# K formed in pairs of steps, sums over rows in pairs, the last chunk's forward transform in column halves, and a new order

## The chip, the cores and the metric

The kernel runs on one core of a Trainium2 chip. The metric is the device time of one execution in microseconds (us), lower is better. The engines are TensorE (PE, whose weight loads are listed as PEld), VectorE (DVE), ScalarE (ACT), GpSimd (POOL), and SyncE (SP), which here issues nearly all transfers.

## The reference

Two state-space convolutions (S4) of the same input are mixed by a gate. L is 2048, D is 512, N is 128.

```python
def _A_ref(u, A_re, A_im, B_re, B_im, C_re, C_im, log_dt, Dskip):   # _B_ref is the same
    dt = jnp.exp(log_dt)[:, None]
    logdA = dt * (A_re + 1j * A_im)
    dB = dt * (B_re + 1j * B_im)
    P = jnp.exp(logdA[:, :, None] * l[None, None, :])
    K = jnp.einsum("dn,dnl,dn->dl", Cc, P, dB).real
    ...  # y = irfft(rfft(u padded to 2 L) * rfft(K padded to 2 L)), first L values
    y = y.transpose(0, 2, 1) + u * Dskip[None, None, :]
    return y

g = _sigmoid((x * gate_w).sum(-1, keepdims=True))
return g * a + (1 - g) * b
```

## The kernel before

Channels come in 8 chunks `c` of 64. A chunk holds its 64 channels for both convolutions, so 128 columns, the first 64 (`s` = 0) for A and the last 64 for B.

**Steps.** A chunk is made in 8 steps `T` of 16 columns, 64 steps in all. In each (`tables`), POOL writes two pieces of phases (`ang`) and two of magnitudes (`mr`, from the seeds `ml` and `mh`), ACT takes two sines and a square (`s`, `ang`, `sq`; `s` and `sq` lie in PSUM), and DVE makes from them the real table in place (`mr`) and the imaginary one (`ei`) with two instructions each (lines 277 and 287). In every fifth step DVE writes one piece of `mr` instead of POOL. PE then forms 4 x 32 rows of K in one PSUM bank (`kgen`, line 595), a copy of 256 values a row takes them to half of `kt`, and an addition of 4 columns puts the skip term in (`kt<-c,dsk`).

**Transforms.** After every second step `first` (line 612) does the first part of K's transform for 32 columns, and two copies put it into `xa` (even chunks) or `xb` (odd ones). When a chunk is complete, `spectrum` (line 625) does the second part in 8 blocks `j`, with the constants `w2` (named `w_0` to `w_3` in the order below), DVE multiplies with the input's spectrum `u` (line 701, result `y`), and `back` does the inverse for two blocks at a time, U = 0 to 3 (line 721). The result goes through `z` to `zb` in DRAM and back in another layout to `f`, for the last chunk to `xa`. The input's spectra were made in the same way at the start (`u_spectra`) and lie in DRAM (`us`).

**Ends.** `fin` (line 757) does the last sums over rows for a quarter `k` of a chunk with constants that carry the gate (`gsi`); a copy of 256 takes them to `o`, and a transfer of 128 KB writes them out. Near the end of the program `stay_awake` runs matmuls without use.

**Start.** The parameters are prepared for groups of one, three and four chunks (`prep`): transposes on PE, then arithmetic on DVE, with two rows on POOL (lines 469 and 498, into `par` or `vv`).

**What sets the order.** Every operation has a number, and the table `ORDER` lists all of them. A word with a `b` takes the second engine of those that it may use (copies: ACT or DVE; the pieces of `mr`: POOL or DVE). Each engine runs its instructions in the order of the table, and SP's transfers wait in line in the same way. Buffers of a ring are given out along the table: `ang` 2, `mr` 3, `ei` 2, `y` 3, `z` 2, `kt` 2, and `c`, 4 PSUM banks of 512 values a row that all matmul results but those in `s` and `sq` share. The last chunk's inverses go to `s` and `sq`, which the steps no longer need.

The functions as they stand before:

Of the kernel before, what the change touches and what calls it, by code (L numbers as in the profile page):

```python
# [207 lines left out]
def ssm_mix(ctx: ExitStack, tc: tile.TileContext, a, out, dry=False):  # L208
    slots, pools, shapes = {}, {}, {}

    def ring(tag, n, shape, dtype=F32, space=None):
# [646 lines left out]
```

## Time and profile before

| | us |
|---|---|
| median of 3 runs | 430.75 (429.98 to 430.92) |
| the profiled execution | 428.49 |
| its span, first to last instruction | 426.7 |
| PE, PEld busy in it | 385.4, 342.9 |
| DVE, ACT, POOL busy | 385.1, 361.4, 359.0 |
| granted TensorE clock | 1.000 |

Busy time is the union of an engine's instructions. An instruction can begin before the one ahead of it has ended, so the durations of a group add up to more than the time that it takes. PE's count of records is twice the count of matmuls in the code. A line named for POOL, DVE or ACT is that of a helper (`tt`, `stt`, `actv`, `copy`), so groups are told apart by their tiles. "Wait" names the engine and line that waited, then what ended the wait, and the us in total, the number and the longest.

### The profile page before, as it was taken

How to read it: one execution, taken by the hardware profiler on the slowest of the kernel's cores; microseconds unless marked ns; L12 is line 12 of the kernel's file. 1: busy time of each engine (PE TensorE's matmuls, PEld its weight loads, DVE VectorE, ACT ScalarE, POOL GpSimd, SP SyncE). 2: the span in 40 equal slices, each digit the busy share in tenths (PEclk: the TensorE clock that was granted, in tenths of full speed). 3: DMA queues.
4: the chain of work that ended last, by engine and by line, in shares of the span. 5: the costliest groups of instructions: out<-in, count | busy, mean ns of one | idle time of the engine just before them, and what ended most of it. 6: DMA issues, size and time to landing. Idle time of an engine off the chain costs nothing.

```text
span 426.7 us, 21919 instructions
## 1 busy us (share of the span) xinstructions
PE 385.4 (90%) x9636; PEld 342.9 (80%) x9636; DVE 385.1 (90%) x547; ACT 361.4 (85%) x522; POOL 359.0 (84%) x291
## 2 busy tenths in 40 slices
PE   5888887799998989999989999999889979999995
PEld 5787776688877878888989988888778968889964
DVE  5799999999999999999989999999999999996620
ACT  2889999999998999999889989999899897992211
POOL 1796999899999999998999999999999999970000
PEclk9999999999999999999999999999999999999999
DMA  8968855078783676588476555674767476567894
GB/s 234 298 207 275 243 169 180 28 230 221 252 248 84 195 228 184 157 243 254 127 226 178 176 173 146 172 232 131 203 220 216 148 233 197 173 196 221 232 269 137
DMA packets 79855, 84.63 MB, mean 198 GB/s; under 512 B 7600, under 2 KB 62768, under 8 KB 79664
## 3 DMA queue, kind: packets, MB, share of 16 engines
q1 hardware_dynamic: 79472, 82.96, 65.0%
q8 instruction: 76, 1.25, 1.2%
q10 hardware_dynamic: 288, 0.26, 0.2%
q14 instruction: 19, 0.16, 0.1%
HBM read 51.55 MB, written 31.65 MB: 195 GB/s over the span
## 4 chain that ended last, share of the span: by engine, by line
PE 34%; ACT 24%; DVE 11%; issue 10%; DMA 9%; POOL 7%; SPq 4%; ACTq 0%; DVEq 0%; POOLq 0%
PE c L612 9%; PE c L625 8%; PE c L595 6%; PE c L721 5%; SPq L295 4%; ACT s L290 4%; ACT sq L290 4%; PE c L757 3%; DVE mr L287 3%; ACT z L300 3%; ACT ang L290 3%; POOL ang L277 3%; DMA zb<-z 2%; POOL mr L277 2%; POOL sa L277 2%
## 5 line engine op out<-in xcount | busy, mean ns | idle before, releaser
L287 DVE SCALAR_TENSOR_TENSOR mr<-sq,mr 128x1024 f32<-128x1024 f32 (+1 forms) x128 | 117.5, 945 | 2.5 <-ACT sq L290 2.4
L277 POOL TENSOR_TENSOR mr<-ml 128x1024 f32<-128x1024 f32 x52 | 101.9, 1960 | 2.0 <-PE c L595 1.5
L277 DVE TENSOR_TENSOR ei<-s,mr 128x1024 f32<-128x1024 f32 x64 | 77.6, 1213 | 2.4 <-POOL mr L277 1.0
L595 PE MATMUL c<-mr 128*32 128x64 f32 x2048 | 64.9, 222 | 8.2 <-DVE mr L287 2.2
L290 ACT ACTIVATE s<-ang 128x1024 f32<-128x1024 int32 x64 | 66.2, 1034 | 5.7 <-DVE ei L287 3.2
L277 POOL TENSOR_TENSOR ang<-sa 128x512 int32<-128x512 int32 x64 | 70.2, 1098 | 0.3
L701 DVE TENSOR_TENSOR y<-c,u 128x1024 f32<-128x1024 f32 x57 | 68.7, 1213 | 1.5 <-PE c L625 1.2
L277 POOL TENSOR_TENSOR ang<-par,cint 128x512 int32<-128x512 int32 x64 | 67.5, 1057 | 2.5 <-ACT sq L290 2.5
L290 ACT ACTIVATE ang<-ang 128x1024 f32<-128x1024 int32 x64 | 67.9, 1060 | 0.9
L277 POOL TENSOR_TENSOR mr<-mh 128x512 f32<-128x512 f32 x64 | 68.6, 1076 | 0.0
L290 ACT ACTIVATE sq<-ang 128x1024 f32<-128x1024 f32 x64 | 66.1, 1033 | 2.9 <-DVE mr L287 1.5
L612 PE MATMUL c<-small,kt 128*64 128x128 f32 x1024 | 63.4, 275 | 2.4 <-ACT z L300 1.4
L595 PE MATMUL c<-ei 128*32 128x64 f32 x2048 | 63.8, 219 | 1.6 <-issue 1.6
L595 PEld LDWEIGHTS c<-mr 128*32 128x32 f32 x2048 | 49.0, 109 | 19.6 <-issue 10.3
L612 PEld LDWEIGHTS c<-small,kt 128*64 128x64 f32 x1024 | 55.6, 137 | 6.3 <-ACT z L300 1.9
L721 PE MATMUL c<-y,vv 64*64 64x128 f32 x1792 | 58.4, 273 | 2.3 <-issue 1.5
L625 PE MATMUL c<-xb,w 128*128 128x128 f32 x384 | 51.8, 283 | 5.1 <-DVE c L420 1.6
L721 PEld LDWEIGHTS c<-y,vv 64*64 64x64 f32 x1792 | 50.5, 133 | 6.9 <-issue 2.9
L625 PE MATMUL c<-xa,w 128*128 128x128 f32 x384 | 53.1, 285 | 3.0 <-ACT z L300 2.3
L625 PEld LDWEIGHTS c<-xb,w 128*128 128x128 f32 x384 | 45.6, 191 | 10.4 <-issue 2.0
L595 PEld LDWEIGHTS c<-ei 128*32 128x32 f32 x2048 | 50.8, 110 | 2.1 <-issue 2.1
L625 PEld LDWEIGHTS c<-xa,w 128*128 128x128 f32 x384 | 46.0, 191 | 7.7 <-ACT z L300 3.0
(108 smaller groups left out, 595.0 us busy)
## 6 DMA issues: line engine op xcount, KB each, us to landing
zb<-z SPq DMA_DIRECT2D x64, 256.0 KB, 3.4
u<-us SPq DMA_DIRECT2D x57, 256.0 KB, 4.1
f<-zb SPq DMA_DIRECT2D x112, 128.0 KB, 3.4
us<-z SPq DMA_DIRECT2D x32, 256.0 KB, 3.4
uin<-in_uk_dram SPq DMA_DIRECT2D x16, 256.0 KB, 4.2
f<-in_ut_dram SPq DMA_DIRECT2D x8, 512.0 KB, 5.6
out_dram<-o SPq DMA_DIRECT2D x28, 128.0 KB, 3.2
par<-prd SPq DMA_DIRECT2D x7, 320.0 KB, 3.4
```

Of the source, the lines that this page charges most:

```text
L277: lambda e: (dve if e == "dve" else pool).tensor_tensor(out=out(), in0=in0(), in1=in1(), op=o),
L287: lambda _: dve.scalar_tensor_tensor(out=out(), in0=in0(), scalar=s, in1=in1(), op0=o0, op1=o1), reads, writes, port=port)
L290: op("act", "act", n, lambda _: act.activation(out=out(), in_=in_(), func=func, **{k: v() if callable(v) else v for k, v in kw.items()}), ...
L295: lambda e: (sp if e == "sp" else act).dma_start(out=out(), in_=in_()), reads, writes, touch=touch)
L300: act.activation(out=o(), in_=i(), func=AF.Copy)
L595: pe.matmul(ps[32 * j:32 * j + 32, o], x[:, 4 * o + j, 64:96], x[:, 4 * o + j, 0:64], start=part == 0, stop=part == 1, tile_position=(0, 3 ...
L612: pe.matmul(t(*ps[g // 4])[64 * r:64 * r + 64, 128 * (g % 4):128 * (g % 4) + 128], t(*x)[:, g], t("small")[:, 128 * r:128 * r + 128], star ...
L625: pe.matmul(view()[:, :, k], t("w2", j // 2)[:, 4 * (j % 2) + k], t(*x1)[:, 4 * j + k], start=True, stop=True)
L701: op("dve", "tt1", 1024, lambda _: dve.tensor_tensor(out=t(*y).rearrange("p h s f d -> p h s (f d)"), in0=fv().rearrange("p s f d -> p s ( ...
L721: pe.matmul(bank_of(x)[64 * e:64 * e + 64, CH * q:CH * q + CH], v[:, 0:64] if h else v[:, 32:96], t(*ys[f // 4])[64 * x:64 * x + 64, h, :, ...
L757: pe.matmul(t(*ps)[64 * r:64 * r + 64, DC * i:DC * i + DC], t("gsi")[:, 4 * k + i, s, 64 * r:64 * r + 64], t(*f)[:, 8 * k + 2 * i + r, DC ...
```

## The change

1. **K in pairs.** Both steps of a pair write their rows into one bank of `c`: the even step takes it, the odd step fills the other half. One copy of 512 and one addition of 8 columns follow the odd step. Before, each step had a bank, a copy of 256 and an addition of 4.
2. **Sums over rows in pairs.** For all chunks but the last, `fin` writes two quarters into one bank, followed by one copy of 512 and one transfer of 256 KB. The outputs use the ring `uin`, which has 3 buffers instead of 2; the ring `o` is gone. The gates' rows in `gsi` stand in another order, so that one DVE instruction of 512 does what two of 256 did. The last chunk keeps quarters of 256, in the order 1, 0, 3, 2. SP now issues all outputs; before, ACT issued two near the end.
3. **Column halves.** The columns s = 0 of the last chunk are complete after four of its eight steps. For the blocks j = 0 to 5, `in_halves` transforms them separately: `fwa` does the first half of two blocks into one bank, and a copy keeps it in a buffer of `uin` or `par`; `fwh` does the second half. A multiplication of each half follows, the kept half on POOL or DVE, the other on DVE. The blocks 6 and 7 stay whole.
4. **The last inverse** uses two banks of `c` instead of `sq`, and the matmuls of `stay_awake` write to `sq`. The last chunk's rows come back to `xa` as four rows of 1024 values for each partition, with one value of space between them; before, as one row of 4096.
5. **The order.** All of `ORDER` is new from its 61st word on, since operations have new numbers and places.

At the start, POOL prepares the first chunk (`prep`, line 498 before and 496 after, is the row that waits for DVE's angle). Before:

```order
L277 TENSOR_TENSOR sa<-par,cint 128x384
L277 TENSOR_TENSOR sa<-par,cint 128x1152
L277 TENSOR_TENSOR ang<-par,cint 128x16x32
L469 TENSOR_TENSOR par<-par,cint 128x128
L498 TENSOR_TENSOR par<-par,y 128x128
L277 TENSOR_TENSOR ang<-par,cint 128x16x32
L277 TENSOR_TENSOR sa<-sa,par 128x32x4
L277 TENSOR_TENSOR ang<-sa 128x16x32
```

and now:

```order
L275 TENSOR_TENSOR sa<-par,cint 128x384
L275 TENSOR_TENSOR ang<-par,cint 128x16x32
L275 TENSOR_TENSOR sa<-par,cint 128x1152
L467 TENSOR_TENSOR par<-par,cint 128x128
L275 TENSOR_TENSOR ang<-par,cint 128x16x32
L496 TENSOR_TENSOR par<-par,y 128x128
L275 TENSOR_TENSOR sa<-sa,par 128x32x4
L275 TENSOR_TENSOR ang<-sa 128x16x32
```

A piece of phases for the second step (`ang<-par,cint`) moved ahead of the row `par<-par,y`, and the first step's piece ahead of the longer `sa`.

Later, POOL writes two rows for the group of four chunks, the second of which (line 498 before, 496 after, into `vv`) takes what DVE writes in `vv<-gsi`. Before:

```order
L277 TENSOR_TENSOR ml_191<-par,small 128x128x8
L277 TENSOR_TENSOR ang<-par,cint 128x16x32
L277 TENSOR_TENSOR ang<-sa 128x16x32
L277 TENSOR_TENSOR mr<-mh_194 128x16x32
L277 TENSOR_TENSOR ang<-par,cint 128x16x32
L277 TENSOR_TENSOR mr<-ml_192 128x16x64
L277 TENSOR_TENSOR mr<-mh_194 128x16x32
L498 TENSOR_TENSOR vv_200<-vv_200,vv_199 128x512
```

and now:

```order
L467 TENSOR_TENSOR vv_196<-vv_196,cint 128x512
L275 TENSOR_TENSOR ang<-par,cint 128x16x32
L275 TENSOR_TENSOR ang<-sa 128x16x32
L275 TENSOR_TENSOR mr<-ml_188 128x16x64
L275 TENSOR_TENSOR ang<-par,cint 128x16x32
L275 TENSOR_TENSOR ang<-sa 128x16x32
L275 TENSOR_TENSOR mr<-mh_190 128x16x32
L496 TENSOR_TENSOR vv_196<-vv_196,vv_195 128x512
```

Before, POOL has written the phases of 9 steps ahead of this row, and DVE's row that it takes stands behind 8 steps' first row of `ei`. Now it is 11 steps on POOL and 9 on DVE.

At the end of the program, on PE, from the last `first` to the sums after the last inverse. Before:

```order
L612 MATMUL c<-small,kt 64x128 x16
L721 MATMUL c<-y,vv_200 64x128 x32
L625 MATMUL c<-xb,w_0_195 128x2x64 x8
L625 MATMUL c<-xb,w_1_196 128x2x64 x8
L721 MATMUL s<-y,vv_199 64x128 x32
L625 MATMUL c<-xb,w_2_197 128x2x64 x8
L721 MATMUL sq<-y,vv_199 64x128 x32
L625 MATMUL c<-xb,w_3_198 128x2x64 x8
L721 MATMUL s<-y,vv_200 64x128 x32
L757 MATMUL c<-f,gsi 64x64 x16
L721 MATMUL sq<-y,vv_200 64x128 x32
L757 MATMUL c<-f,gsi 64x64 x32
```

and now, up to the third inverse (then a final sum, and the last inverse into `c`):

```order
L711 MATMUL c<-xb,w_0_191 64x64 x8
L711 MATMUL c<-xb,w_1_192 64x64 x8
L711 MATMUL c<-xb,w_0_191 64x64 x8
L711 MATMUL c<-xb,w_1_192 64x64 x16
L749 MATMUL s<-y,vv_195 64x128 x32
L711 MATMUL c<-xb,w_1_192 64x64 x8
L711 MATMUL c<-xb,w_2_193 64x64 x8
L625 MATMUL c<-xb,w_3_194 128x2x64 x4
L749 MATMUL sq<-y,vv_195 64x128 x32
L711 MATMUL c<-xb,w_2_193 64x64 x8
L625 MATMUL c<-xb,w_3_194 128x2x64 x4
L749 MATMUL s<-y,vv_196 64x128 x32
```

The rows of 64x64 are the halves; x16 is one `fwa` of two blocks, x8 one `fwh`. The `fwa` for j = 0, 1 and for j = 4, 5 stand further up, ahead of the last but one and ahead of the last `first`.

The diff; `ORDER` with its first changed line alone:

```diff
...
-35 36 180 181 40 41 42 43 44 45 47 46 183 184 79 182 76 9 187 8 7 80 78 336 215 360 48 49 50 186 185 51 52 55 56 82 83 84 61
...
+35 36 180 181 40 41 42 43 44 45 47 46 183 184 79 182 76 9 185 186 80 187 360 7 78 336 338 8 223 215 49 48 50 51 82 52 56 55 62
...
-    ring("xa", 1, [128, F1, CH])
+    ring("xa", 1, [128, 4 * (8 * CH + 1)])
-    ring("uin", 2, [128, 8, L2])
+    ring("uin", 3, [128, 8, L2])
...
-    ring("o", 2, [128, 4, DC])
...
-        kc, kt = ("c", "time", T), ("kt", T // 2)
+        kc, kt = ("c", "time", T // 2), ("kt", T // 2)
+        kv = lambda: t(*kc).rearrange("p (x l) -> p x l", l=L2)
...
-                        pe.matmul(ps[32 * j:32 * j + 32, o], x[:, 4 * o + j, 64:96], x[:, 4 * o + j, 0:64],
+                        pe.matmul(kv()[32 * j:32 * j + 32, 4 * (T % 2) + o], x[:, 4 * o + j, 64:96], x[:, 4 * o + j, 0:64],
                                   start=part == 0, stop=part == 1, tile_position=(0, 32 * j))
-        op("pe", "kgen", 128, kgen, [M, E], [kc], table="kgen")
-        copy(256, lambda: t(*kt)[:, 4 * (T % 2):4 * (T % 2) + 4], lambda: t(*kc)[:, 0:256].rearrange("p (o l) -> p o l", o=4), [kc], [kt])
-        tt("dve", 4, lambda: t(*kt)[:, 4 * (T % 2):4 * (T % 2) + 4, 0], lambda: t(*kc)[:, 0:256].rearrange("p (o l) -> p o l", o=4)[:, :, 0],
-           lambda: t("dsk", c)[:, g], OP.add, [kc, kt, ("dsk", c)], [kt], port=False)
+        op("pe", "kgen", 128, kgen, [M, E], [kc] if T % 2 == 0 else [kc, ("kc2", T)], table="kgen")
         if T % 2:
+            copy(512, lambda: t(*kt), kv, [kc], [kt])
+            tt("dve", 8, lambda: t(*kt)[:, :, 0], lambda: kv()[:, :, 0],
+               lambda: t("dsk", c)[:, g - 1:g + 1].rearrange("p a b -> p (a b)"), OP.add, [kc, kt, ("dsk", c)], [kt], port=False)
             first(("k", T), kt, (("xa", "xb")[c % 2], c), G * (g - 1))
...
+        half = [("xh", k0 // DC)] * (x1[1] == NCH - 1)
         op("pe", "wide", 64, mm, [x, ("small",)], [*ps, x1], table="fin")
...
-                    for P in range(2):
-                        dve.scalar_tensor_tensor(
...
+                    dve.scalar_tensor_tensor(
+                        out=t("gsi")[:, 4 * n:4 * n + 4, s], in0=t(*ps).rearrange("p (i l) -> p i l", i=4), scalar=1.0,
+                        in1=t("small")[:, 256 + 128 * s:384 + 128 * s].unsqueeze(1).to_broadcast([128, 4, 128]),
+                        op0=o, op1=OP.mult)
...
         fv = lambda: t(*fw).rearrange("p (s f d) -> p s f d", s=2, f=4)
+        if c == NCH - 1 and j < NJ - 2:
+            in_halves(c, j, x1, fw, y, uk, uv)
+            return
         spectrum(x1, j, fw, fv)
...
+    def columns(x1, j, s, out):
+        for k in range(4):
+            for r in range(2):
+                pe.matmul(out[64 * r:64 * r + 64, DC * k:DC * k + DC], t("w2", j // 2)[:, 4 * (j % 2) + k, 64 * r:64 * r + 64],
+                          cube(x1)[:, 4 * j + k, DC * s:DC * s + DC], start=True, stop=True, tile_position=(0, 64 * r))
+
+    def in_halves(c, j, x1, fw, y, uk, uv):
+        P = j // 2
+        ps, kept = ("c", "early", P), (("uin", "early", 0), ("uin", "early", 1), ("par", "early"))[P]
...
+        if j % 2 == 0:
+
+            def mm(_):
+                for i in range(2):
+                    columns(x1, j + i, 0, t(*ps)[:, 256 * i:256 * i + 256])
+
+            op("pe", "fwa", 64, mm, [("xh", 0), ("w2", P)], [ps], table="fin", touch=[x1])
+            copy(512, kv, lambda: t(*ps), [ps], [kept])
+        op("pe", "fwh", 32, lambda _: columns(x1, j, 1, t(*fw)), [("xh", 1), ("w2", P)], [fw], table="fin", touch=[x1])
+        yv = lambda s: t(*y)[:, :, s].rearrange("p h f d -> p h (f d)")
+        spread = lambda v: v.unsqueeze(1).to_broadcast([128, 2, 4 * DC])
+        tt("any", 512, lambda: yv(0), lambda: spread(kv()[:, 256 * (j % 2):256 * (j % 2) + 256]),
+           lambda: uv().rearrange("p h f d -> p h (f d)"), OP.mult, [kept, *uk], [y])
+        tt("dve", 512, lambda: yv(1), lambda: spread(t(*fw)[:, 0:256]), lambda: uv().rearrange("p h f d -> p h (f d)"), OP.mult,
+           [fw, *uk], [("yb", c, j)], port=False, touch=[y])
+
...
-        ps = [(("s", "sq")[U % 2], "inv", U)] if last else [("c", "inv", c, U, x) for x in range(2)]
-        bank_of = lambda x: t(*ps[0]).rearrange("p a b -> p (a b)")[:, 512 * x:512 * x + 512] if last else t(*ps[x])
+        wide = last and U < 3
+        ps = [(("s", "sq")[U % 2], "inv", U)] if wide else [("c", "inv", c, U, x) for x in range(2)]
+        bank_of = lambda x: t(*ps[0]).rearrange("p a b -> p (a b)")[:, 512 * x:512 * x + 512] if wide else t(*ps[x])
...
+        both = [("yb", c, 2 * U + i) for i in range(2)] * (last and U < 3)
+        op("pe", "inv", 128, inv, [*ys, *both, ("vv", U // 2)], ps, table="square")
...
-        whole = last and U < 3
-        for h in range(1 if whole else 4):
-            a0, an = (0, 32) if whole else (8 * h, 8)
-            dma(512 if whole else 128, lambda a0=a0, an=an: t(*f).rearrange("(r u) a k -> u r a k", u=4)[U, :, a0:a0 + an],
-                lambda a0=a0, an=an: t(*zb)[8 * U:8 * U + 8].rearrange("g (m a) k -> (g m) a k", m=4)[:, a0:a0 + an],
-                [("zu", c, U, 0), ("zu", c, U, 1)],
...
+        if last and U < 3:
+            dma(512, lambda: rows_of(eighths(f), U)[:, :, 0:8 * CH],
+                lambda: t(*zb)[8 * U:8 * U + 8].rearrange("g (m h a) k -> (g m) h (a k)", m=4, h=4),
+                [("zu", c, U, 0), ("zu", c, U, 1)], [f] * new + [("fu", c, U, i) for i in range(4)], touch=[zb] + [f] * (not new))
+            return
...
+    def gated_row(x):
+        return 4 * (x % 8 // 2) + 2 * (x // 8) + x % 2
...
-        late = c == NCH - 1 and k >= 2
-        f, ps, o = home(c), ("c", "fin", c, k), ("uin", "late", k) if late else ("o", c, k)
+        last, P, h = c == NCH - 1, k // 2, k % 2
+        f, ps, o = home(c), ("c", "fin", c, k) if last else ("c", "fin", c, P), ("uin", "o", c, P)
+        at = 0 if last else 4 * h
...
-        op("pe", "fin", 64, mm, [("gsi", n) for n in ((0, 1), (2, 3))[k % 2]] + [("fu", c, U, k) for U in range(4)], [ps], table="fin", touch=[f])
-        copy(256, ov, lambda: t(*ps)[:, 0:256].rearrange("p (i d) -> p i d", i=4), [ps], [o])
-        dma(128, lambda: out[:, c, 4 * k:4 * k + 4], ov, [o], (), c >= NCH - 2)
+                        pe.matmul(pv()[64 * r:64 * r + 64, at + i], t("gsi")[:, gated_row(4 * k + i), s, 64 * r:64 * r + 64],
+                                  turned_rows(f, k, 2 * i + r)[:, DC * s:DC * s + DC], start=s == 0, stop=s == 1, tile_position=(0, 64 * r))
+        op("pe", "fin", 64, mm, [("gsi", n) for n in ((0, 1), (2, 3))[k % 2]] + [("fu", c, U, k) for U in range(4)],
+           [ps] if last or h == 0 else [("sums", c, P)], table="fin", touch=[f] if last or h == 0 else [f, ps])
+        if last:
+            copy(256, lambda: t(*o)[:, 4 * h:4 * h + 4], lambda: pv()[:, 0:4], [ps], [o] if h else [("oh", c, k)], [] if h else [o])
+            dma(128, lambda: out[:, c, 4 * k:4 * k + 4], lambda: t(*o)[:, 4 * h:4 * h + 4], [o if h else ("oh", c, k)], (), True, touch=[o])
+        elif h:
+            copy(512, lambda: t(*o), pv, [ps, ("sums", c, P)], [o])
+            dma(256, lambda: out[:, c, 8 * P:8 * P + 8], lambda: t(*o), [o], (), c == NCH - 2)
...
-        ps = ("c", "awake")
+        ps = ("sq", "awake")
...
-        for k in range(4):
+        for k in (0, 1, 2, 3) if c < NCH - 1 else (1, 0, 3, 2):
             fin(c, k)
...
```

More of the change, by code (lines that the diff above doesn't have):

```diff
@@ L156 @@
+1884 1892 1896 1899b 1897 1900 1890 1893 1891 1894
 """
@@ L236, in ssm_mix @@
         "logdt": [128, NCH],
-        "dummy": [128, 1], "small": [128, 525], "gsi": [128, 16, 2, 128], "gate_w": [128, 4],
+        "small": [128, 525], "gsi": [128, 16, 2, 128], "gate_w": [128, 5],
         "dt": [128, 3, NCH], "ex": [128, NCH], "ek": [128, NCH], "er": [128, NCH], "ea": [128, NCH]}
@@ L613, in mm @@
                               t("small")[:, 128 * r:128 * r + 128], start=True, stop=True, tile_position=(0, 64 * r))
+        half = [("xh", k0 // DC)] * (x1[1] == NCH - 1)
         op("pe", "wide", 64, mm, [x, ("small",)], [*ps, x1], table="fin")
         for h in range(2):
[L617 to L618 removed]
+            copy(512, lambda h=h: cube(x1)[:, :, k0 + 16 * h:k0 + 16 * h + 16].rearrange("p f (g j) -> p f g j", j=4),
+                 lambda h=h: t(*ps[h]).rearrange("p (g f j) -> p f g j", g=4, j=4), [ps[h]], [x1] + half)
     def spectrum(x1, j, fw, view):
@@ L624, in mm @@
             for k in range(4):
-                pe.matmul(view()[:, :, k], t("w2", j // 2)[:, 4 * (j % 2) + k], t(*x1)[:, 4 * j + k], start=True, stop=True)
+                pe.matmul(view()[:, :, k], t("w2", j // 2)[:, 4 * (j % 2) + k], cube(x1)[:, 4 * j + k], start=True, stop=True)
         op("pe", "fwd", 16, mm, [x1, ("w2", j // 2)], [fw], table="full")
@@ L723, in inv @@
                                       tile_position=(64 * x, 64 * e))
-        op("pe", "inv", 128, inv, [*ys, ("vv", U // 2)], ps, table="square")
+        both = [("yb", c, 2 * U + i) for i in range(2)] * (last and U < 3)
+        op("pe", "inv", 128, inv, [*ys, *both, ("vv", U // 2)], ps, table="square")
         z, zb, f = ("z", c, U), ("zb", c), home(c)
         for x in range(2):
-            copy(512, lambda x=x: t(*z)[:, x].rearrange("p q k -> p (q k)"), lambda x=x: bank_of(x), [ps[0 if last else x]],
+            copy(512, lambda x=x: t(*z)[:, x].rearrange("p q k -> p (q k)"), lambda x=x: bank_of(x), [ps[0 if wide else x]],
                  [z] * (x == 0) + [("zx", c, U, x)], [z] * x)
@@ L734, in back, with rows_of, eighths, turned_rows @@
                 [("zx", c, U, x)], [zb] * (new and x == 0) + [("zu", c, U, x)], touch=[z] + [zb] * (not (new and x == 0)))
-        whole = last and U < 3
-        for h in range(1 if whole else 4):
-            a0, an = (0, 32) if whole else (8 * h, 8)
-            dma(512 if whole else 128, lambda a0=a0, an=an: t(*f).rearrange("(r u) a k -> u r a k", u=4)[U, :, a0:a0 + an],
-                lambda a0=a0, an=an: t(*zb)[8 * U:8 * U + 8].rearrange("g (m a) k -> (g m) a k", m=4)[:, a0:a0 + an],
-                [("zu", c, U, 0), ("zu", c, U, 1)],
-                [f] * (new and h == 0) + [("fu", c, U, i) for i in (range(4) if whole else (h,))],
-                touch=[zb] + [f] * (not (new and h == 0)))
+        if last and U < 3:
[3 more added lines that the diff above has]
+            return
+        for h in range(4):
+            dma(128, lambda h=h: rows_of(eighths(f), U)[:, h, 0:8 * CH] if last else
+                rows_of(t(*f), U)[:, 8 * h:8 * h + 8].rearrange("p a k -> p (a k)"),
+                lambda h=h: t(*zb)[8 * U:8 * U + 8].rearrange("g (m a) k -> (g m) a k", m=4)[:, 8 * h:8 * h + 8].rearrange("p a k -> p (a k)"),
+                [("zu", c, U, 0), ("zu", c, U, 1)], [f] * (new and h == 0) + [("fu", c, U, h)],
+                touch=[zb] + [f] * (not (new and h == 0)))
+    def rows_of(tile_view, U):
+        return tile_view.rearrange("(r u) a k -> u r a k", u=4)[U]
+    def eighths(f):
+        return t(*f).rearrange("p (h x) -> p h x", h=4)
+    def turned_rows(f, k, a):
+        return t(*f)[:, 8 * k + a] if f[0] == "f" else eighths(f)[:, k, CH * a:CH * a + CH]
+    def cube(x):
+        return t(*x)[:, 0:F1 * CH].rearrange("p (f k) -> p f k", k=CH) if x[0] == "xa" else t(*x)
+    def gated_row(x):
+        return 4 * (x % 8 // 2) + 2 * (x // 8) + x % 2
     def home(c):
```

83 lines of the change are left out of this document (39 added, 44 removed), and 76 rows, old and new, of the table ORDER.

## The prediction

> **What bounds the kernel now.** I read the page's busy line first, then the busy time by stretch, POOL's waits, and the end of the program engine by engine. The busy line of the page:
>
> ```profile
> PE 385.4 (90%) x9636; PEld 342.9 (80%) x9636; DVE 385.1 (90%) x547; ACT 361.4 (85%) x522; POOL 359.0 (84%) x291
> ```
>
> No engine stands out over the whole span, so the stretch decides. In the next view the columns are start and end, length, then busy us (and instructions) of PE, PEld, DVE, ACT and POOL, the granted clock, the DMA share and GB/s:
>
> ```profile
> 20.00:60.00 40.00, 33.89 (x564) 30.97 (x560) 37.92 (x58) 37.78 (x55) 35.68 (x29) 1.00 0.78 242
> 60.00:380.00 320.00, 295.90 (x8005) 263.76 (x8003) 313.45 (x420) 299.75 (x424) 312.86 (x248) 1.00 0.63 187
> 380.00:427.00 47.00, 41.60 (x936) 35.43 (x924) 21.27 (x27) 12.84 (x24) 1.61 (x2) 1.00 0.71 209
> ```
>
> From 60 to 380 us DVE is idle for 6.6 us and POOL for 7.1, ACT for 20.3, PE for 24.1. So the loop over the steps is held by two engines at 98%, and its end follows POOL's, whose work this change leaves as it is. What POOL can give back is its waits (total, times, longest):
>
> ```profile
> POOL ml L277 <- DMA gsi<-in_pk_dram: 8.7, 1, 8.7
> POOL vv L498 <- DVE vv L426: 5.8, 2, 3.8
> POOL ang L277 <- ACT sq L290: 2.5, 4, 1.3
> POOL par L498 <- DVE y L426: 2.1, 1, 2.1
> POOL mr L277 <- PE c L595: 1.5, 3, 0.9
> ```
>
> The first is the load at the start, which stays. The other 11.9 us are the most that the loop can give. Then the end, in order of time (start, length):
>
> ```profile
> 380.53 1.08 POOL L277 TENSOR_TENSOR mr<-mh 128x512 f32<-128x512 f32 x1
> 384.58 1.81 DVE L287 SCALAR_TENSOR_TENSOR mr<-sq,mr 128x1024 f32<-128x1024 f32 x2
> 388.65 1.97 PE L612 MATMUL c<-small,kt 128*64 128x128 f32 x32
> 390.55 1.98 PE L721 MATMUL c<-y,vv 64*64 64x128 f32 x64
> 392.46 3.84 PE L625 MATMUL c<-xb,w 128*128 128x128 f32 x32
> 406.99 1.98 PE L721 MATMUL sq<-y,vv 64*64 64x128 f32 x64
> ```
>
> and, in the chain of waits, what follows the last inverse:
>
> ```profile
> 409.73 0.69 DVE z L302
> 410.44 4.60 DMA zb<-z
> 417.21 2.86 DMA xa<-zb
> 420.20 2.10 PE c L757 x64
> 422.38 0.38 ACT o L300
> ```
>
> POOL ends at 381.6, the last DVE table at 386.4, the last inverse at 409.0, and 17.7 us of copies, transfers and sums follow. So there are three terms: POOL's waits in the loop, PE's work from 386.4 to 409.0, and the transfers after it.
>
> **The change part by part.** The groups that are removed or added, with their mean ns:
>
> ```profile
> L300 ACT ACTIVATE kt<-c 128x256 f32<-128x256 f32 x52 | 19.8, 382 | 3.7 <-PE c L595 3.5
> L302 DVE COPY kt<-c 128x256 f32<-128x256 f32 x12 | 5.0, 413 | 0.7 <-PE c L595 0.7
> L277 DVE TENSOR_TENSOR kt<-c,dsk 128x4 f32<-128x4 f32 x64 | 9.9, 155 | 1.3 <-ACT kt L300 1.1
> L300 ACT ACTIVATE z<-c 128x512 f32<-128x512 f32 x74 | 42.3, 596 | 7.2 <-PE c L721 4.7 <-PE c L625 0.9 <-DMA us<-z 0.8
> L302 DVE COPY z<-c 128x512 f32<-128x512 f32 x14 | 9.4, 681 | 2.6 <-PE c L721 2.5
> L300 ACT ACTIVATE o<-c 128x256 f32<-128x256 f32 x21 | 7.9, 382 | 11.6 <-DMA out_dram<-o 9.4 <-PE c L757 2.2
> L677 DVE SCALAR_TENSOR_TENSOR gsi<-c,small 128x256 f32<-128x256 f32 x16 | 5.6, 412 | 0.0
> L701 DVE TENSOR_TENSOR y<-c,ml 128x1024 f32<-128x1024 f32 x4 | 4.7, 1219 | 1.5 <-PE s L721 1.1 <-PE c L625 0.4
> L277 POOL TENSOR_TENSOR mr<-mh 128x512 f32<-128x512 f32 x64 | 68.6, 1076 | 0.0
> ```
>
> Means overstate what a short instruction costs, because the next one begins before it ends. These starts show it:
>
> ```profile
> 366.43 0.38 ACT L300 ACTIVATE kt<-c 128x256 f32<-128x256 f32 x1
> 366.69 0.60 ACT L300 ACTIVATE xb<-c 128x512 f32<-128x512 f32 x1
> 367.17 1.04 ACT L290 ACTIVATE s<-ang 128x1024 f32<-128x1024 int32 x1
> 367.90 0.15 DVE L277 TENSOR_TENSOR kt<-c,dsk 128x4 f32<-128x4 f32 x1
> 367.97 0.68 DVE L287 SCALAR_TENSOR_TENSOR mr<-sq,mr 128x512 f32<-128x512 f32 x1
> ```
>
> A kt addition holds DVE for 0.07 us, not 0.155; a copy of 256 holds ACT for 0.26, one of 512 for 0.48.
>
> DVE, loop: 32 additions fewer, 32 x 0.07 = 2.2 us (5.0 by the mean, the upper end). Copies to kt and to the outputs go from 21 of 256 to 7 of 512 and one of 256, but four whole copies to z and xb and one to vv come over from ACT: about 0.3 us less. The gates' rows: 5.6 us become 8 x 0.68 = 5.4. Together 2.5 to 3 us less.
>
> ACT, loop: two copies of 256 cost 2 x 0.26 = 0.52 and one of 512 costs 0.48, so batching gives 0.04 x 28, about 1 us; the five copies handed to DVE give 2.6 more, the three new copies of early halves take 1.5 back. ACT had 20.3 us idle, so this counts only where POOL waits for ACT.
>
> PE: a whole forward transform of one j takes 3.84 / 4 = 0.96 us. A half is 8 matmuls of the shape of the final sums, whose 64 records take 2.10, hence 16 records 0.53; two halves are 1.05. Nothing is saved: six j cost 0.5 us more in all. Only the place changes. Bounds of a half, since no such matmul exists: 0.48 to 0.53.
>
> POOL: four new multiplications of halves, priced by the nearest row at 1.08 each, behind its last table; POOL is idle there. What covers them: PE's forward halves of the other columns. Without that cover the inverses would wait for them.
>
> SP: the outputs of seven chunks go from 28 transfers to 14, and two that ACT issued come to SP. The three pieces of 512 KB to xa are cut in four rows each, at offsets 4 bytes apart from round ones. No row has that shape; the nearest is the piece to xa issued behind all three, which lands 2.86 us after 417.21. I take 0, with 0 to 1 us as bounds.
>
> **Term 1, POOL's waits.** At the start the new order puts one more ang row ahead of the row that waited 2.1 us for DVE; the row takes about 1.0, so 1.0 of the wait goes. The row that waited the smaller part of the 5.8 us (5.8 - 3.8 = 2.0) now has 11 steps of POOL's work ahead of it where DVE's row has 9, before 9 against 8. That is one step more of cover, and even one `mr` row of it is 1.08, so the 2.0 is gone. The 3.8 us wait stands as it did. The waits for ACT and PE (2.5 + 1.5 = 4.0) are reached by lighter ACT and DVE; I take a quarter, 1.0. That makes 4.0. DVE must follow: it has 6.6 us idle plus 2.5 of work gone, so it can, but its order is as rigid as POOL's, and I take off 0.5: 3.5 us. Bounds: 0 (other waits appear) and 10 (nearly all of 11.9 goes).
>
> **Term 2, PE at the end.** From 392.46 to 409.0 PE runs eight forward transforms, four inverses and one final sum without a gap, 16.5 us. In the new order six halves (3.2), one pair of early halves (1.05), two whole transforms (1.9), four inverses (7.6) and a final sum (1.1) stand there, 14.9: 1.6 less. Against it: the last y can be written only when the third inverse has freed its buffer, and the 1.22 us on DVE are covered by 1.1 of PE's, 0.15 late; the last kt copy is 596 on ACT instead of 413 on DVE, 0.2 late; and the 2.1 us moved ahead of 386.4 need a place in a PE that is dense there, paid from 24.1 us of idle time earlier. I take 1.0, with 0 and 2 as bounds.
>
> **Term 3, transfers.** Both copies to z now stand on DVE (two of 0.68) where one was on ACT, but before, too, the second began at 409.73, after the first. The final sums run in the order 1, 0, 3, 2, and one output still stands on SP between the last pieces. I take 0, between -0.5 and +1.
>
> Sum: -3.5 - 1.0 = -4.5 us. The profiled execution took 428.49 us (span 426.7), 2.3 below the median of the runs, 430.75; it would be 424.0, and the median 426.2.
>
> One rule of the skill speaks against the new multiplications. Two rows bear on it, the same DVE operation once with an input in PSUM and once with two inputs in SBUF:
>
> ```profile
> L432 DVE SCALAR_TENSOR_TENSOR gsi<-c,gsi 128x512 f32<-128x512 f32 x2 | 1.4, 678 | 0.0
> L432 DVE SCALAR_TENSOR_TENSOR gsi<-gsi 128x512 f32<-128x512 f32 x1 | 1.0, 984 | 0.0
> ```
>
> The second took 306 ns longer with POOL at work beside it. The Trainium skill (SBUF — State Buffer, Who interferes with whom) says that a DVE instruction with two SBUF inputs contends with a GpSimd instruction reading SBUF, and that the loser blocks for the other's whole length. The two rows agree in sign. By the rows two halves would cost 2 x 0.31 = 0.6 us (426.8), by the rule two whole POOL halves (C). The y halves from kept copies have two SBUF inputs, two of them on DVE while POOL does four.
>
> **Rivals.**
> A, all waits go: POOL loses nearly all of its 11.9 us, capped by DVE (6.6 idle here, 2.1 from 20 to 60, 2.5 to 3 of work gone, so 11), and the end gains 1.6. For it: the sum of POOL's work allows it. Against it: buffers of two and three steps tie POOL to the others. About -10: 420.7.
> B, it does not do what it says: POOL is as full as before, the batching saves work on engines that wait for it, and PE's halves move into a PE that has no room. -1 to 0: 429.7 to 430.8.
> C, as forecast, but the two DVE halves with both inputs in SBUF each wait for one POOL half, 2 x 1.08 = 2.2 us at the end: -4.5 + 2.2, 428.4.
> D, slower: the sums of a pair now sit in one of four PSUM banks from the first step's matmuls to the copy after the second's, one step longer. PE's present waits for banks look like this:
>
> ```profile
> PEld c L625 <- ACT z L300: 2.5, 4, 0.9
> PEld c L625 <- ACT xa L300: 1.9, 5, 0.7
> PEld c L625 <- ACT o L300: 1.8, 2, 1.4
> PEld c L612 <- ACT z L300: 1.9, 2, 1.4
> ```
>
> These are 8.1 us from 60 to 380. If they double, PE loses 8.1 of its 24.1 us of slack, and of that I put three quarters on the path: 6 us on top of the forecast, 432.2. It decides once PE's added waits on the path pass 4.5 us. For it: PE has no gap in the rows of the end, and little slack to take a wait. Against it: one copy and the wait for it are gone from every pair.
>
> **How the numbers follow.** Forecast 0.42 (424 to 428), A 0.15, B 0.14, C 0.07, D 0.22. A difference under 0.2% (0.9 us) is about what a measurement of this kernel cannot tell from none. Faster: 0.42 + 0.15 + 0.07 + 0.05 of B = 0.69; same: 0.08 of B; slower: D and the rest of B, 0.23. The range from 420.5 to 432 leaves out about half of A and half of D, under 0.2.
>
> **What the changed profile would show.** Right: POOL's last table ends 3 to 4 us earlier in the span; its wait for vv is one of about 3.8 instead of two; 32 additions of 8 columns near 0.155 us; the last inverse 21 to 22 us after the last DVE table instead of 22.6. Wrong: new waits of PE for banks ahead of the step's matmuls or of first's (D); DVE halves over 0.9 us (C); POOL's last table at the same time with waits in new places (B); or transfers to xa of 512 KB that PE's final sums wait for.

## The result: 1.4% slower, 436.7 us against 430.8

The changed kernel takes 436.71 us (median of 4 runs, 435.62 to 437.14) and the kernel before 430.84 us beside it (429.98 to 432.29). The ratio is 1.0136, with a 95% interval of 1.0096 to 1.0176. The profiled execution took 436.79 us with a span of 435.0. The forecast was 426.2 us, and its range ended at 432.0.

The page of the changed kernel, busy line, and the three stretches that the prediction showed of before (same columns):

```profile
PE 387.2 (89%) x9780; PEld 343.9 (79%) x9780; DVE 382.1 (88%) x501; ACT 360.8 (83%) x487; POOL 364.3 (84%) x295
```

```profile
20.00:60.00 40.00, 32.06 (x539) 28.94 (x539) 36.59 (x56) 36.08 (x53) 35.12 (x30) 1.00 0.74 237
60.00:380.00 320.00, 292.90 (x7850) 261.85 (x7850) 307.54 (x371) 294.35 (x386) 307.86 (x244) 0.99 0.60 181
380.00:435.00 55.00, 48.13 (x1246) 40.94 (x1241) 25.05 (x34) 18.51 (x30) 11.61 (x10) 1.00 0.68 208
```

DVE has 3.0 us less work over the span, near the forecast, and ACT 0.6, where the forecast's parts came to about 2. But from 60 to 380 us all four engines did less in the same time: DVE 5.9 us, ACT 5.4, POOL 5.0, PE 3.0, though POOL's work was not changed. POOL's waits (total, times, longest):

```profile
POOL ml L275 <- DMA gsi<-in_pk_dram: 8.5, 1, 8.5
POOL ang L275 <- ACT sq L288: 8.3, 8, 2.6
...
POOL vv L496 <- DVE vv L424: 5.5, 2, 3.1
...
POOL par L496 <- DVE y L424: 1.5, 1, 1.5
POOL mr L275 <- DVE c L418: 1.4, 1, 1.4
POOL mr L275 <- PE c L594: 1.1, 1, 1.1
```

The wait for ACT's square went from 2.5 us to 8.3. The end in order of time, POOL's and DVE's last table first, then PE:

```profile
385.41 1.08 POOL L275 TENSOR_TENSOR mr<-mh 128x512 f32<-128x512 f32 x1
392.10 1.81 DVE L285 SCALAR_TENSOR_TENSOR mr<-sq,mr 128x1024 f32<-128x1024 f32 x2
393.37 1.97 PE L611 MATMUL c<-small,kt 128*64 128x128 f32 x32
...
396.30 1.34 PE L711 MATMUL c<-xb,w 128*64 128x64 f32 x32
...
401.22 2.55 PE L711 MATMUL c<-xb,w 128*64 128x64 f32 x80
...
405.63 1.15 PE L711 MATMUL c<-xb,w 128*64 128x64 f32 x32
...
409.71 0.69 PE L711 MATMUL c<-xb,w 128*64 128x64 f32 x16
...
414.06 1.15 PE L805 MATMUL c<-f,gsi 128*64 128x64 f32 x32 [0.67 <-PE s L749]
415.14 1.98 PE L749 MATMUL c<-y,vv 64*64 64x128 f32 x64
```

and the last links of the chain of waits:

```profile
415.05 6.27 DMA zb<-z
421.38 4.47 DMA xa<-zb
426.79 4.17 PE c L805 x128
```

Against the profile before, in us from one mark to the next:

| | before | changed | |
|---|---|---|---|
| POOL's last table ends | 381.6 | 386.5 | +4.9 |
| from there to DVE's last table | 4.8 | 7.4 | +2.6 |
| from there to the end of the last inverse | 22.6 | 23.2 | +0.6 |
| from there to the end of the span | 17.7 | 17.9 | +0.2 |

These 8.3 us are more than the medians' 5.9, because the profiled execution of before was 2.3 us faster than its median; its granted clock was 1.000, that of the changed kernel's 0.992.

### The profile page after: what moved, and what is told of

Its sections match the earlier page's. It is cut to its first block, busy times and chain, and to the rows that moved or that the text cites. A ratio compares the mean times of both kernels' runs of the same rounds, so it can differ in the third digit from the quotient of the medians.

```text
span 435.0 us, 22106 instructions
## 1 busy us (share of the span) xinstructions
PE 387.2 (89%) x9780; PEld 343.9 (79%) x9780; DVE 382.1 (88%) x501; ACT 360.8 (83%) x487; POOL 364.3 (84%) x295
## 4 chain that ended last, share of the span: by engine, by line
PE 36%; ACT 17%; POOL 14%; DVE 12%; DMA 10%; issue 9%; SPq 2%; DVEq 0%; ACTq 0%; POOLq 0%
PE c L625 8%; PE c L611 8%; POOL mr L275 6%; PE c L749 6%; PE c L594 6%; POOL ang L275 6%; PE c L805 4%; DMA zb<-z 3%; DVE mr L285 3%; ACT s L288 2%; DVE y L702 2%; SPq L293 2%; ACT ang L288 2%; DVE ei L275 2%; ACT mh L529 2%
## 5 line engine op out<-in xcount | busy, mean ns | idle before, releaser
L594 PE MATMUL c<-mr 128*32 128x64 f32 x2048 | 63.8, 222 | 11.0 <-DVE mr L285 7.6
L275 POOL TENSOR_TENSOR ang<-sa 128x512 int32<-128x512 int32 x64 | 69.2, 1081 | 0.2
L749 PE MATMUL c<-y,vv 64*64 64x128 f32 x1856 | 59.5, 273 | 3.4 <-DVE y L702 1.8
L749 PEld LDWEIGHTS c<-y,vv 64*64 64x64 f32 x1856 | 51.5, 133 | 8.8 <-DVE y L702 2.9
L298 ACT ACTIVATE z<-c 128x512 f32<-128x512 f32 x74 | 42.1, 593 | 11.5 <-PE c L749 8.9
L625 PE MATMUL c<-xb,w 128*128 128x128 f32 x336 | 47.1, 287 | 2.1 <-ACT z L298 0.9
```

Source lines behind the costliest of these rows:

```text
L275: lambda e: (dve if e == "dve" else pool).tensor_tensor(out=out(), in0=in0(), in1=in1(), op=o),
L298: act.activation(out=o(), in_=i(), func=AF.Copy)
L594: pe.matmul(kv()[32 * j:32 * j + 32, 4 * (T % 2) + o], x[:, 4 * o + j, 64:96], x[:, 4 * o + j, 0:64], start=part == 0, stop=part == 1, til ...
L625: pe.matmul(view()[:, :, k], t("w2", j // 2)[:, 4 * (j % 2) + k], cube(x1)[:, 4 * j + k], start=True, stop=True)
L749: pe.matmul(bank_of(x)[64 * e:64 * e + 64, CH * q:CH * q + CH], v[:, 0:64] if h else v[:, 32:96], t(*ys[f // 4])[64 * x:64 * x + 64, h, :, ...
```

## Experiments

Every ratio is to the kernel before, run on the same chip in the same session, with its 95% interval. One per cent is 4.3 us.

**Edits and order apart.** Four kernels put the one's operations into the other's order. Operations without a counterpart were placed by rule, and an operation that found no buffer was put off to the first place that had one.

```diff
 # e1: changed operations, ORDER of before       # e2: before + K in pairs only, ORDER of before
-        kc, kt = ("c", "time", T), ("kt", T // 2)
+        kc, kt = ("c", "time", T // 2), ("kt", T // 2)
 # e3: changed kernel, K by the step again, ORDER as changed     # e4: and sums, halves, last inverse as before
-        kc, kt = ("c", "time", T // 2), ("kt", T // 2)
+        kc, kt = ("c", "time", T), ("kt", T // 2)
```

> All edits, in the order of the kernel before. Where a bank of c, held for a pair, is not free at the old place, the operation waits for the first place in the table where it is; the new operations (early halves, halves of y) stand beside the ones they replace. Theory O (the order is what costs: waits chained between ACT, PE and DVE): 427 to 431.5, like before or a little faster. Theory K (the bank held one step longer costs, wherever it stands): 434 or more, with PE's waits for banks at least doubled from 8 us. Theory T (the column halves and the cut rows of the last chunk cost at the end): last table on POOL at 381 to 382 as before, but more than 45.3 us from there to the end.

> The kernel before with K in pairs alone (one bank, one copy of 512, one addition of 8 for two steps); everything else and the order as before, save that operations that find no free bank are put off to the first place that has one. Theory O: 429.5 to 431, the batching gives ACT and DVE some 3 us of work back that POOL does not turn into time. Theory K: 433 or more, since 4 banks with one held for a pair make PE and its readers wait. Theory T: as before, 430 to 431.

> The changed kernel with K by the step again (a bank, a copy of 256 and an addition of 4 for each step; those of the even step 7 and 10 places behind its matmuls), all other edits and the order as changed. Theory O: 435 to 438, no better than the changed kernel. Theory K: 431 to 433, most of the loss gone. Theory T: 435 to 437.

> The new order with the edits taken back as far as buffers allow: K by the step, sums over rows by the quarter, whole forward transforms of the last chunk, last inverse into sq. What stays of the edits: the ring for the outputs with 3 buffers, the gates' rows by 512, the last chunk's rows cut in four, the quarters 1, 0, 3, 2. Theory O: 434 to 438. Theory K: 430 to 432. Theory T: 430 to 432.5, the end as before.

Measured: 1.0851 (1.0763 to 1.0939), 1.0309 (1.0235 to 1.0383), 1.0953 (1.0839 to 1.1067) and 1.1289 (1.1196 to 1.1383). Theory K's "434 or more" and "433 or more" cover the first two, but by K the third had to take 431 to 433 us, and it took 469. No theory fits the four. The third, waits:

```profile
POOL ang L277 <- ACT sq L290: 31.1, 15, 4.4
DVE kt L277 <- ACT kt L300: 24.8, 14, 4.6
```

An addition placed three places behind its copy holds DVE until ACT reaches that copy. So each table fits only its own operations, and a part moved without a new order measures its bad place. This says nothing on what K in pairs is worth in an order made for it; that stays open. What follows keeps both orders as they are.

**Splices.** At some places of the table both kernels have issued nearly the same operations. There one can run one kernel, operations and order, up to step T, and the other from there on. At 17, 40, 55 and 63 no operation had to be put off, at 24 one load.

```diff
 # e5: before to step 17, then changed        # e6: changed to step 17, then before
+        if T < 18:     # e6: T >= 18
+            kc = ("c", "step", T)            # bank, copy of 256, addition of 4
...
+        else:
+            kc, kt = ("c", "time", T // 2), ("kt", T // 2)       # the pair's bank
...
```

> A splice. Both orders have issued the same set of operations when the matmuls of step 17 stand in the table, so the kernel before (K by the step) runs to there, word for word, and the changed kernel from there on. Theory L (the loss comes in a few places of the order, each named in the trace of the changed kernel: 2.0 us of POOL's work behind by 140 us, 3.3 us from 140 to 180, and 3.3 us after POOL's last table): only the first part goes, 433.5 to 435.5. Theory K (the pair's bank costs in every pair, all along): three quarters of the 6 us stay, 434.5 to 436. Theory S (a wait at the start sets off the one at 150 us): 430 to 432.5.

> The opposite splice: the changed kernel to the matmuls of step 17, the kernel before from there on, with its whole transforms and its end (the ring for outputs keeps 3 buffers, the gates' rows stay by 512). Theory L: 432 to 433.5, the first 2 us. Theory K: 431.5 to 433. Theory S: 434 to 436.

> The kernel before to the matmuls of step 63, the last, and the changed kernel's end from there on: six blocks of the last chunk in column halves, the early halves too, the last inverse in c, the sums in the order 1, 0, 3, 2. The early halves that the changed kernel makes before step 63 stand behind it here. Theory L: the end costs 3.3 us in the changed kernel, 2.6 of it between POOL's and DVE's last table, which step 63's order sets; here 431 to 435. Forecast of the record: the end is 1 us shorter, 429.8 or less.

> The changed kernel to the matmuls of step 63, then the end of the kernel before: whole transforms, the last inverse in sq, quarters in the order 0, 1, 2, 3. No early halves anywhere. Theory L: 433 to 436.5, the 5.3 us of the loop stay and some of the 3.3 of the end go. Theory that the column halves are the loss: 431 to 433.

Measured: e5 1.0078 (1.0050 to 1.0106), e6 1.0003 (0.9977 to 1.0030), e7 1.0039 (1.0010 to 1.0067), e8 1.0074 (1.0041 to 1.0106). By itself the start of the changed order costs nothing (e6), the loop after step 17 about 3 us, and the new end 1.7 us more; e7 and e8 add up to 1.1%, inside the interval of the whole. One run does not fit well: e5 has the changed loop and the changed end and loses 0.78%, less than the whole's 1.36, and the intervals only just meet. Whether the start takes a share after all when the changed loop follows it stays open.

> Splice: the changed kernel to the matmuls of step 40 (about 260 us), the kernel before from there on. With the splice at 17 there was no loss, with that at 63 3.1 us. If the loss grows evenly with the steps: half, 1.3 to 2. If it sits in the stretch after 180 us where PE idles 1.8 us more: all of it here, 2.5 to 3.5. If it sits near the end of the loop: under 0.8.

> Splice: the changed kernel to the matmuls of step 55 (about 345 us), the kernel before from there on. Evenly grown: 2.3 to 2.8 us over the kernel before. Loss near 200 us: 2.5 to 3.5. Loss in the last eight steps, where early halves and whole copies crowd PE and ACT: under 1.

> Splice: the changed kernel to the matmuls of step 24 (about 170 us), the kernel before from there on. The splice at 17 cost nothing, that at 40 about 4 us. If the stretch around the seeds of chunk 4 (185 to 200 us, where ACT takes 12.3 to 12.8 us from square to square in the changed order and 10.5 before) is the loss: 430 to 432. If the loss comes from 130 to 170 us (waits of 0.6 for a square at 140 and 1.3 for PE at 161): 433 to 435.

Measured: 1.0098 (1.0053 to 1.0144), 1.0090 (1.0058 to 1.0122) and 1.0116 (1.0069 to 1.0162). So with the changed order kept to step 24, 40, 55 or 63 the loss is about the same, 0.7 to 1.2%, and with step 17 it is nil. So what sets it off stands in steps 18 to 25 of the changed order, between 130 and 170 us, and it does not grow. "Near the end of the loop" and "evenly with the steps" both fall.

The traces show where POOL pays for it. The 17th and the 33rd of POOL's 64 rows `mr<-mh`, of before, of e7 (the same program to step 63) and of the changed kernel:

```profile
124.98 1.07 POOL L277 TENSOR_TENSOR mr<-mh 128x512 f32<-128x512 f32 x1
215.42 1.07 POOL L277 TENSOR_TENSOR mr<-mh 128x512 f32<-128x512 f32 x1
```

```profile
127.89 1.07 POOL L279 TENSOR_TENSOR mr<-mh 128x512 f32<-128x512 f32 x1
218.75 1.06 POOL L279 TENSOR_TENSOR mr<-mh 128x512 f32<-128x512 f32 x1
```

```profile
125.65 1.09 POOL L275 TENSOR_TENSOR mr<-mh 128x512 f32<-128x512 f32 x1
221.08 1.09 POOL L275 TENSOR_TENSOR mr<-mh 128x512 f32<-128x512 f32 x1
```

From the one to the other: 90.4 and 90.9 us in the old order, 95.4 in the new. From the 33rd to the last it is 165.1, 165.7 and 164.3, no loss at all. Most of the delay comes after 170 us: in e17, which has the old order again from there, POOL's 17th to 25th row take 42.4 us and the 25th to the 33rd 51.4, in before 41.0 and 49.4. The first row of e7 is as telling: identical code was 2.9 us later than in the profile before, so a single profile of this kernel is good to about 3 us. The last section shows what made these 2.9 us.

**The same again, and less work for PE.**

```diff
-                for s in range(2):
+                for s in range(1 if c == 5 else 2):      # e10; e9 is unaltered
...
```

> The changed kernel once more, unaltered, for a second profile and a time beside the runs below. 434 to 437. In its first profile TensorE stood idle at 76.6 us (3.0) and 151.4 us (2.2), each followed by matmuls at a lower clock. If the program sets both, they are there again; if the one at 151, which no operation ended, is chance, it is gone, and POOL's last table comes 1.5 to 2 us earlier than at 386.5.

> The changed kernel, which leaves out half of the matmuls of chunk 5's sums over rows (64 of 128 in the code; 128 of 256 records, about 2.2 us of PE between 372 and 380 us). Theory P (PE is what the end follows, already before POOL's last table): 1.5 to 2.5 us less than the changed kernel, and the lag from POOL's to DVE's last table goes from 7.4 to about 5.5. Theory G (POOL's tables set the end, as the record has it): within 0.5 us of the changed kernel, the lag unchanged.

Measured: e9 1.0149 (1.0099 to 1.0199), e10 1.0046 (1.0005 to 1.0086). The last tables of e10, to set beside 386.5 and 393.9:

```profile
386.01 1.08 POOL L275 TENSOR_TENSOR mr<-mh 128x512 f32<-128x512 f32 x1
...
390.38 1.81 DVE L285 SCALAR_TENSOR_TENSOR mr<-sq,mr 128x1024 f32<-128x1024 f32 x2
```

POOL is where it was, DVE's last table ends 5.1 us after it instead of 7.4 (7.7 in e9). The seven other profiles with the changed loop and end have 6.7 to 7.7. From POOL's last table to the end of the last inverse it is 27.9 us, in the changed kernel 30.6 and in e9 30.5. Theory P holds: at the end the kernel follows PE. The times alone would not decide it: the medians of all executions differ by 2.2 us, what was taken out, the ratios by 4.4, with wide intervals. Of e9's two gaps the one at 73 us is there (3.0 us), and so is the one at 150 us, now 1.51 long and ended by DVE, without a slower clock behind it. It is not chance: of twelve profiles with the changed order in this stretch ten show PE idle for 1.2 us or more from 148.7 to 151.3 us on. Of four with the old order none does; two have 1.2 us a little later (151.7 and 155.3), ended by DVE's real table. POOL's last table came no earlier, at 388.0.

**The wait at 199 us.** The largest of POOL's waits for ACT in the loop, ACT in e9, from one square to the next:

```profile
185.92 1.03 ACT L288 ACTIVATE sq<-ang 128x1024 f32<-128x1024 f32 x1
186.91 1.09 ACT L298 ACTIVATE z<-c 128x512 f32<-128x512 f32 x2
188.02 1.28 ACT L529 ACT_TABLE_LOAD   x1
...
192.83 0.58 ACT L298 ACTIVATE z<-c 128x512 f32<-128x512 f32 x1
193.43 1.28 ACT L288 ACT_TABLE_LOAD   x1
...
198.22 0.60 ACT L298 ACTIVATE z<-c 128x512 f32<-128x512 f32 x1 [1.38 <-DMA zb<-z]
198.71 1.02 ACT L288 ACTIVATE sq<-ang 128x1024 f32<-128x1024 f32 x1
```

It takes 12.8 us here and 10.5 in the same place of before: the seeds of chunk 4 (exponentials with two loads of tables) stand between copies of three inverses. Two edits take copies away, e13 by one word of the table and e18 by the engine of four:

```diff
 ORDER, a stretch                   # e13: 1492 is the copy to z, 783 the square of step 27
-1492 783 785 1493b 798
+783 1492 785 1493b 798
 # e18: 1462, 1463, 1478 and 1492 become 1462b, 1463b, 1478b, 1492b (DVE)
```

> The changed kernel with one word of the table moved: on ACT, the copy to z of chunk 2's second inverse stands behind the square of step 27 instead of ahead of it. In the changed kernel that copy waits 1.4 us near 197 us for a transfer that still reads the z buffer, the square waits behind it, and POOL waits 2.6 to 3.1 us for the square at 199. If this wait is the loop's loss (theory Z): POOL's wait there falls by 1.5 to 2, its last table ends that much earlier, and the kernel takes 434.5 to 435.5. If the loss only looks for another place: within 0.8 us of the changed kernel.

> The changed kernel with the four copies to z that ACT has between the squares of steps 25 and 27, around the seeds of chunk 4, given to DVE at the same places. From square to square ACT then takes 9.4 us instead of 12.3 to 12.8. If ACT's work there is the loss: POOL's wait of 1.8 to 3.2 us at 199 falls under 1, its last table ends 2 to 3 us earlier, and the kernel takes 434 to 435. If DVE then becomes late instead: POOL or PE waits for DVE there, and the time is within 0.8 us of the changed kernel's.

Measured: 1.0107 (1.0040 to 1.0173) and 1.0125 (1.0072 to 1.0179), no better than the changed kernel. In e18 ACT no longer has any copy there, and POOL:

```profile
197.09 1.03 ACT L288 ACTIVATE sq<-ang 128x1024 f32<-128x1024 f32 x1 [1.98 <-DVE mr L285]
198.26 1.05 POOL L275 TENSOR_TENSOR ang<-par,cint 128x512 int32<-128x512 int32 x1 [2.00 <-ACT sq L288]
204.15 1.05 POOL L275 TENSOR_TENSOR ang<-par,cint 128x512 int32<-128x512 int32 x1 [0.88 <-ACT sq L288]
208.71 1.05 POOL L275 TENSOR_TENSOR ang<-par,cint 128x512 int32<-128x512 int32 x1 [1.46 <-ACT sq L288]
```

The square now waits for DVE, and 4.3 us of waits stand where e9 had 3.8. So the wait at 199 only shows a delay that lies further back, as the splice at 24 says. What makes it between 130 and 170 us is not settled. The trace offers one candidate, again e9:

```profile
151.33 1.12 PE L669 MATMUL c<-uin,small 128*128 128x512 f32 x2 [1.51 <-DVE y L702]
152.49 1.29 DVE L676 SCALAR_TENSOR_TENSOR gsi<-c,small 128x512 f32<-128x512 f32 x2 [1.59 <-PE c L669]
154.19 0.58 ACT L298 ACTIVATE kt<-c 128x512 f32<-128x512 f32 x1
155.74 1.09 ACT L298 ACTIVATE z<-c 128x512 f32<-128x512 f32 x2 [0.97 <-PE c L749]
```

PE has just filled a pair's bank (to 149.8), and ACT empties it only at 154.2, behind the exponentials. PE waits for another bank, DVE for PE, ACT for PE and POOL for ACT. This was not tried. Against it stands e5: with the changed order in this stretch PE has no gap over 0.8 us from 142 to 160 us there, and POOL still takes 95.8 us from its 17th to its 33rd row.

**The gap at 73 us.** In every profile of the changed kernel PE stands idle for 3.0 us there.

```diff
 ORDER, a stretch                   # 257, 258: the copies to xb; 155, 159, 158: rows of prep on ACT; 466: a sine
-155 159 158 466 263 255 256 257 258
+263 255 256 257 258 155 159 158 466
```

> The changed kernel with the first two copies to xb of the third input transform moved ahead of three rows of the parameter work on ACT (near 73 us). TensorE stood idle for 3.0 us there in every profile of the changed kernel, until these copies freed their banks, and the 32 matmuls behind the gap took 3.5 to 3.7 us where 1.97 is usual. Expected: the gap shrinks to 1 to 1.5 us, the matmuls take 1.97, the granted clock stays at 1.00 there. If what PE loses there reaches the end: 1.5 to 3 us faster than the changed kernel; if POOL's later waits absorb it: within 0.8.

> Both moves in the changed kernel. If the two losses add: 3 to 4.5 us faster than the changed kernel, 432 to 434. What the end costs (2 to 3 us) stays.

> The splice at step 17 (changed kernel first, then the kernel before), which took as long as the kernel before, with the copies to xb moved ahead of the parameter work as in the run on that alone. If the gap of 3.0 us at 74.8 and the slow matmuls behind it (clock 0.61 and 0.70) cost time to the end: 428 to 429.5, faster than both kernels. If not: 430 to 431.

Measured: 1.0115 (1.0054 to 1.0175), 1.0162 (1.0105 to 1.0219), 1.0032 (0.9997 to 1.0066). The move failed. In e16:

```profile
72.28 2.88 PE L631 MATMUL c<-small,uin 128*64 128x128 f32 x48 [0.55 <-DVE kt L277]
79.53 0.32 PE L613 MATMUL c<-mr 128*32 128x64 f32 x8 [4.37 <-ACT xb L300]
```

The next matmuls start at once, but then PE is held behind them, for 4.37 us instead of 3.0, and the clock falls all the same (0.77 from 78 to 82). Since the gap was not removed, it stays open what it costs. No version here beats both kernels: e6 is level with the one before.

## Why the prediction was wrong

**"Its end follows POOL's."** No run speaks against it in the loop; at the end it does not hold. e10 shows that PE's work of 372 to 380 us reaches the end.

**Term 1, POOL's waits, was -3.5 and is about +3** (e8, 0.74%; +4.9 in the profiles). Behind the first load POOL's waits came to 11.9 us before, were to become 7.9, and became 17.8. Row by row: the wait in `par` lost 0.6 instead of 1.0. The smaller wait for vv did not go (5.5 - 3.1 = 2.4 us are left, before 2.0): the step of POOL's work that now stands ahead of it covered nothing, so DVE's row came later as well. The step that failed is the quarter: waits for ACT and PE of 4.0 us were to fall to 3.0, because those engines have less to do, and they became 9.4 (8.3 + 1.1). Less work on ACT did not make its squares earlier. They come when the instruction ahead of them in ACT's order is done, and that waits for PE or a transfer. I read the order around the rows that POOL waits for, and not around the squares.

**Term 2, PE at the end, was -1.0 and is +3.2** in the profiles (2.6 + 0.6). The prices held: the 128 records of halves behind the last chunk-6 inverse take 4.4 us by their rows (2.55 + 1.15 + 0.69; forecast 3.2 + 1.05), and from 401.22 to the end of the last inverse it is 15.9 us, 0.67 of them idle, where before had 16.5. What failed is the sentence that the 2.1 us of early halves are paid from PE's idle time elsewhere. That idle time lies between waits that the order sets. The last matmuls of K start 1.36 us after DVE's last table (395.27), because PE is still at `first`; before, 0.14 us. And DVE's last table is late itself, because ACT had waited 2.34 us for PE (at 385.4) ahead of the square before it. Even behind step 63 the halves don't pay: e7 costs 1.7 us, and from POOL's last table to the end of the last inverse it takes 29.1 us, 27.4 before and 30.6 in the changed kernel. But the halves are not all of the +3.2: e8, which has none of them, takes 29.3 us there, so that up to 1.9 come with the changed loop.

**Term 3, transfers, was 0 and is +0.2.** Right, though the last links differ: 6.27 and 4.47 us against 4.60 and 2.86, in e9 5.00 and 3.41. In the changed profile the 6.27 carry the third inverse's result, and the last sums wait for its piece of 512 KB, a sign that the prediction had named; in e9, as before, the last links are those of the last inverse.

**Rivals.** A and B fall with term 1. C falls here: the DVE halves with both inputs in SBUF take 0.69, since POOL rests in that moment. POOL's halves, priced at 1.08, take 1.27 to 1.29. D named the right sign and mostly the wrong mechanism. PE's waits for DVE's real tables grew, from 60 to 380 us, before and changed:

```profile
PE c L595 <- DVE mr L287: 2.2, 4, 1.2
```

```profile
PE c L594 <- DVE mr L285: 6.0, 10, 1.0
```

Its waits for copies by ACT, from which D was priced, did not double: all rows of weight loads (PEld) that end with one add up to 12.3 us before, of which the prediction had summed four, and 12.6 now. The place at 149 us is the one that fits D, with e5 against it. Its time, 432, was low by 4.7 us.

## To carry to other kernels

Where each engine runs a fixed list, an instruction saved gives time only if the instruction that someone waits for comes earlier; follow the late one back along its own engine's list before you count a saving. Find out which engine the end follows by taking work from it (e10), not by its idle time, which may lie where it can't be used. And take a second profile before subtracting two: equal code differed by 3 us here, because the granted clock did; compare it stretch by stretch.

## What the runs showed of the hardware

The clock of TensorE fell in or just behind gaps of 2 to 4 us, and then stood at 0.50 for 3.41 us or twice that. In e9 this came with the gap of 3.02 us (6.83 us from 75.5 on), and in e7 with one of 2.38 us at 56.5 (6.83 us from 58.2 on):

```profile
74.00:78.00 4.00, 1.57 (x16) 1.58 (x18) 4.00 (x7) 3.97 (x7) 4.00 (x5) 0.69 0.21 67
78.00:82.00 4.00, 3.30 (x68) 2.90 (x67) 4.00 (x6) 2.71 (x4) 4.00 (x4) 0.50 0.02 4
```

```profile
58.00:62.00 4.00, 3.10 (x14) 3.10 (x15) 2.78 (x5) 2.80 (x5) 3.20 (x3) 0.53 0.45 142
```

The same gap of 2.43 us left it at 1.00 in the profile before and lowered it in e5 (0.61 from 78 to 82), and one of 2.76 us in e7 did nothing. The Trainium skill (TensorE: Matmul & The Clock Gate, Part 1) states a window of about 3.4 us that runs freely, and half the clock after an idle one. That the outcome changes with the moment agrees, and so do the 3.41 us; that 2.1 to 2.4 us of idle time are enough does not follow from it, and the rows decide.

What it costs can be read in e7: its rows on POOL are level with those of before up to 60.2 us and 2.9 us late from 72.3 on, with the 6.83 us at half the clock between. Over 91 executions of the kernel before, the median is 429.4 us where the mean granted clock was 0.9965 or more and 432.6 where it was under 0.9895. The changed kernel's ten average 0.9915, those of before 0.9937. By a line fitted to the 91 (0.33 us for each 0.001) that makes some 0.7 us of its 6, an estimate; so the clock is at most a small part of what makes it slower.

A DVE multiplication with both inputs in SBUF takes 0.69 us alone. Beside POOL's halves, in e7:

```profile
399.42 0.94 DVE L279 TENSOR_TENSOR y<-par,mh 128x512 f32<-128x512 f32 x1 [1.97 <-ACT par L302]
403.80 0.99 DVE L279 TENSOR_TENSOR y<-uin,ml 128x512 f32<-128x512 f32 x1 [1.64 <-PE s L771]
398.53 2.96 POOL L279 TENSOR_TENSOR y<-uin,ml 128x512 f32<-128x512 f32 x2 [12.98 <-DMA f<-zb]
402.97 1.27 POOL L279 TENSOR_TENSOR y<-uin,ml 128x512 f32<-128x512 f32 x1 [1.48 <-DMA f<-zb]
```

DVE lost 0.25 to 0.30 us each time, close to the 0.31 of the prediction's rows, and POOL 0.4 over the first two (1.27 alone). POOL's first half ended at 399.81 and its third at 404.24, and both DVE rows ended 0.55 us after that; of the prediction's row of 984 ns the end (84.07) came 0.54 us after POOL's (83.53). So DVE seems to have done its work only when POOL's instruction was over. The Trainium skill (SBUF — State Buffer, Who interferes with whom) lets the one that comes second wait until the first has ended. The trace agrees, and the price was small because POOL's instruction had only some 0.4 us left when DVE's came. What two that start together cost, as C had it, no run here shows.
